# Last group's h on VectorE ahead of P7's T, streamed weights made behind each T's product, and T2 behind k^T v's addition

## The chip, the cores and the metric

The kernel runs on one core of one Trainium2 chip. The metric is the device time in microseconds of one execution. Before the change it is 1124.7 us, the median of three runs (1122.6 to 1124.93). The profile of the kernel before is of one execution and covers 1121.9 us from the first instruction to the last; every time "at" which something happens below is counted from the start of that span.

The core's engines are named as the profile names them: PE is TensorE (matrix products; PEld is its loading of weights), DVE is VectorE, ACT is ScalarE, POOL is GpSimd, and SP is SyncE, which here only issues transfers.

## The reference, cut to what matters

Linear attention with a normalised output is followed by a SwiGLU feed-forward block.

```python
# q, k, v: (8 batches, 8 heads, 576, 64)
kv  = einsum('bhsd,bhse->bhde', k, v)            # k^T v, 64x64 for each head
out = einsum('bhsd,bhde->bhse', q, kv)
out = out / sqrt(mean(out * out, -1) + 1e-6) * g_norm
x   = out.transpose(0, 2, 1, 3).reshape(4608, 512)

# w_gate, w_val: (512, 1536); w_out: (1536, 512)
h = silu(x @ w_gate) * (x @ w_val)
result = h @ w_out
```

Everything is in float32.

## The kernel before: what the change and the steps touch

The 4608 rows of x are cut into nine blocks of 512 (numbered 0 to 8). For each block there is an "up" part (x times the gate and value weights, then h) and a "down" part (h times the output weights). The attention of the next block is computed in between: its k^T v during up, its q transposed between up and down, its products, norm and transposed x during down.

Block 0 does its up part plainly. All other products are done with a seven-product scheme (Strassen's, in Winograd's form) on 2x2 blocks. The seven products are called P1 to P7. Products that go to the same PSUM buffer are accumulated there:

```python
    CHAIN = {1: ("b", True), 6: ("b", False), 7: ("b", False), 4: ("b", False), 2: ("a", True),
             5: ("c", True), 3: ("c", False)}      # PSUM buffer, and whether it begins a sum
```

Three of the weight operands (for P5, P7 and P4) are differences of weight blocks, made on GpSimd and called T. They live in nine buffers (`t_pool`), which are also the buffers into which streamed weights are loaded. T2 is another weight operand, b22 - b12 + b11, made in place.

Block 1 uses one level of the scheme (class `Up`, six units j), and in passing it makes the weights of the second level from the same T and stores them in DRAM. Blocks 2 to 8 use two levels in the up part (class `Inner`: three groups d of four outer products each) and load these weights from DRAM as a stream. The down part always has one level (class `Down`).

The last steps of a group of h in blocks 2 to 8; `HB` is 256 and `BLK` 512:

```python
        def made3(self, p, e, q):                 # class Inner, fourth outer pair (4, 3)
            if p != 4:
                return
            h = self.ffn.h[:, 4 * self.d : 4 * self.d + 4]
            c11, c12, c21, c22 = (self.whole(*i) for i in ((1, 1), (3, 1), (3, 0), (1, 0)))
            mul(nc.gpsimd, h[:, :, 0:HB], c11, c12)
            nc.scalar.activation(out=c21, in_=c21, func=ACT.Silu)
            mul(nc.gpsimd, h[:, :, HB:BLK], c21, c22)
            self.ffn.h_sums(2 * self.d, 2, nc.gpsimd if 4 * self.d + 4 < NF else nc.vector)
```

The down part. P1 reads h's first half, three groups one after the other; P5 reads the sums s1; P7 reads what `turn_s3` leaves in h:

```python
    class Down(Quad):
        ...
        def turn_t(self, p):
            pairs = wo.rearrange("p (j e) d -> p e j d", e=2)
            of = {5: pairs[:, 1, :, HD:DM], 7: pairs[:, 0, :, 0:HD], 4: pairs[:, 1, :, 0:HD]}[p]
            self.t[p] = []
            for i in range(0, NP, 2):
                t = t_tile((self.ffn.n, p))
                sub(nc.gpsimd, t, of[:, i : i + 2], pairs[:, 0, i : i + 2, HD:DM])
                self.t[p] += [t[:, 0], t[:, 1]]
        ...
        def turn_s3(self):
            pairs = self.ffn.h.rearrange("p (j e) t -> p e j t", e=2)
            sub(nc.vector, pairs[:, 0, :, 0:HB], pairs[:, 0, :, HB:BLK], pairs[:, 1, :, HB:BLK])

        def down(self, fill):                     # class Ffn
            down = self.down_
            fill = dict(zip((1, 6, 2), fill))     # steps of the next block's attention
            for p in (1, 5, 6, 7, 2, 4, 3):
                if p == 1:
                    down.turn_t(7)
                if p == 6:
                    down.turn_t(4)
                down.multiply(p)
                self.make(12)
                if p in fill:
                    fill[p]()
                if p == 1:
                    down.turn_s3()
```

The next block's attention: `turn_q` transposes q ahead of P1; the step behind P1 multiplies by k^T v, squares, forms the inverse root (VectorE, eleven small operations) and scales; the step behind P6 begins with `turn_x`, which transposes the scaled x on TensorE.

Block 1's units and what makes the weights of the second level:

```python
    class Up(Quad):
        def sequence(self, last):                 # last: the unit before
            return [(self, 1), (self, 5), (last, 4), (last, 3), (self, 6), (self, 2), (self, 7)]

        def after2(self):
            add(nc.vector, self.s, self.ps["a"], self.s)
            nc.scalar.activation(out=self.s, in_=self.s, func=ACT.Silu)

        def after7(self):
            self.u3 = self.piece(2)
            nc.scalar.copy(out=self.u3, in_=self.ps["b"])
            add(nc.vector, self.u3, self.ps["c"], self.u3)

        def after3(self):
            add(nc.vector, self.u2, self.ps["c"], self.u2)
            mul(nc.gpsimd, self.h[:, :, 0:HB], self.s, self.u2)
            self.ffn.h_sums(self.j, 1, nc.vector)
            if self.ffn.n == DEEP - 1:
                self.ffn.making.extend(leaves(self.j, self.w))
```

`leaves` yields, for each of five sources (three T, and the gate and value weights in pairs), four VectorE operations. It puts all results into one room of 21 blocks of 128x128 (tile xi) and sends a transfer as soon as both of its operands are there, 17 for each unit. Three steps are done after each product in up, twelve in down.

At the end of block 0, behind its down part, the value weights get their T2, and block 1's k^T v has been added up shortly before:

```python
            if js[-1] == NS - 1:                  # Att.kv
                dst = kvs[self.n % 3]
                nc.scalar.copy(out=dst, in_=self.kv_ps[0])
                add(nc.vector, dst, self.kv_ps[1], dst)
    ...
        if n == 0:
            with tc.issue_after(ended.ins):
                for j in range(NP):
                    t2(wv[j][:, 0:2], wv[j][:, 2:4], wg[j][:, 0:2])
```

A scheduler lays down the order in which each engine gets its instructions; the program's order is what it starts from.

Of the kernel before, what the change touches and what calls it, by code (L numbers as in the profile page):

```python
# [8 lines left out]
F32 = mybir.dt.float32  # L9
# [5 lines left out]
P = 128  # L15
# [3 lines left out]
def kernel(  # L19
# [41 lines left out]
    nc = tc.nc  # L61

    B, H, S, D = q.shape
    NT, DM = out.shape
    FF = moe_w_gate.shape[1]
    T = 4
    BLK = P * T
    HB = BLK // 2
    HD = DM // 2
    NB = NT // BLK  # L70
    NS = DM // P
    NF = FF // P
# [12 lines left out]
    x_pool = pool("x", 1)  # L85
# [28 lines left out]
    def ring():  # L114

        return r_pool.tile([P, 4, BLK], F32, name="r")
# [67 lines left out]
    class Att:  # L184
# [57 lines left out]
        def kv(self, js):  # L242


            if self.n == B:
                return
            if js[0] == 0:
                self.kv_ps = [m_psum.tile([P, NS, D], F32, name="m") for _ in range(2)]
            for j in js:
                for c in range(KT):  # L250
                    for r in range(2 if c < KT - 1 else 1):
                        rows = slice(r * D, (r + 1) * D)
                        for u in range(2):
                            nc.tensor.matmul(  # L254
                                self.kv_ps[r][u * D : (u + 1) * D, j, :], lhsT=self.k[j][rows, u, c, :],
                                rhs=self.v[j][rows, u, c, :], start=(c == 0), stop=(c == KT - 1 - r),
                            )
            if js[-1] == NS - 1:
                dst = kvs[self.n % 3]
                nc.scalar.copy(out=dst, in_=self.kv_ps[0])  # L260
                add(nc.vector, dst, self.kv_ps[1], dst)

        def turn_q(self, i, pools=None):

            if i == 0:
                self.qt = ring().rearrange("p t (j c) -> p t j c", j=NS)
            for t in (2 * i, 2 * i + 1):
                pool = pools[t % 2] if pools else m_psum
                ps = pool.tile([P, NS, P], F32, name=pool.name[0])
                for j in range(NS):  # L270
                    nc.tensor.transpose(ps[:, j], self.q[t][:, j], ident)
                if t % 2 or self.n == 1:
                    nc.scalar.copy(out=self.qt[:, t], in_=ps)
                else:
                    nc.vector.tensor_copy(out=self.qt[:, t], in_=ps)
# [103 lines left out]

        def turn(self):  # L380
            for i in range(2):
                self.turn_q(i, (m_psum, b_psum))

        def steps(self):

# [20 lines left out]
    DEEP = 2  # L406

    class Quad:
# [9 lines left out]
        def multiply(self, p):  # L418
            name, first = CHAIN[p]
            if first:  # L420
                self.ps[name] = PSUMS[name].tile([P, 2, HB], F32, name=name)
            for e, i in self.order(p):
                lhsT, rhs = self.operands(p, e, i)

                nc.tensor.matmul(  # L425
                    self.ps[name][:, e], lhsT=lhsT, rhs=rhs, start=first and (e, i) == (0, 0),
                    stop=i == self.steps - 1, skip_group_check=True,
                )
            getattr(self, f"after{p}", lambda: None)()
# [17 lines left out]
    class Up(Quad):  # L447
# [36 lines left out]
        def after3(self):  # L484
            add(nc.vector, self.u2, self.ps["c"], self.u2)
            mul(nc.gpsimd, self.h[:, :, 0:HB], self.s, self.u2)
            self.ffn.h_sums(self.j, 1, nc.vector)
            if self.ffn.n == DEEP - 1:
                self.ffn.making.extend(leaves(self.j, self.w))

    class Inner:

# [100 lines left out]
        def made3(self, p, e, q):  # L593
            if p != 4:
                return
            h = self.ffn.h[:, 4 * self.d : 4 * self.d + 4]
            c11, c12, c21, c22 = (self.whole(*i) for i in ((1, 1), (3, 1), (3, 0), (1, 0)))
            mul(nc.gpsimd, h[:, :, 0:HB], c11, c12)
            nc.scalar.activation(out=c21, in_=c21, func=ACT.Silu)
            mul(nc.gpsimd, h[:, :, HB:BLK], c21, c22)  # L600
            self.ffn.h_sums(2 * self.d, 2, nc.gpsimd if 4 * self.d + 4 < NF else nc.vector)


    RESIDENT = (1, 6, 2, 3)
    QUARTER = {1: (0, 0), 6: (0, 1), 2: (1, 0), 3: (1, 1)}

    CHUNKS = (
        ((5, 1), (5, 6)), ((1, 5), (5, 5)), ((5, 2), (5, 3)), ((1, 7), (5, 7)), ((6, 5), (2, 5)), ((1, 4), (5, 4)),
        ((6, 7), (2, 7)), ((7, 1), (7, 6)), ((7, 7), (7, 5)), ((6, 4), (2, 4)), ((7, 2), (7, 3)), ((4, 1), (4, 6)),
        ((4, 5), (3, 5)), ((7, 4),), ((4, 2), (4, 3)), ((4, 7), (3, 7)), ((4, 4), (3, 4)),  # L610
    )

# [40 lines left out]
        stream.held.append(key)  # L653
        return t_pool.tile([P, 2, 2 * P], F32, name="t")

    made = {}

    def leaves(j, w):


        if not made:
            made["room"] = x_pool.tile([P, 3, 7, P], F32, name="xi").rearrange("p a b c -> p (a b) c")
        room = made["room"]
        d, f = divmod(j, 2)
        two = lambda b: room[:, b : b + 14].rearrange("p (o r) c -> p o r c", o=2)

        sources = []
        for o, b, r in ((5, 1, 2), (7, 18, 1), (4, 12, 2)):
            sources.append((w[o].unsqueeze(1), (o,), room[:, b : b + 2 * r + 1 : 2 * r].unsqueeze(1),
                            room[:, b + r].unsqueeze(1)))  # L670
        for t, os, b in ((wg, (1, 2), 0), (wv, (6, 3), 6)):
            sources.append((t[j].rearrange("p (o i) c -> p o i c", o=2), os, two(b)[:, :, 0:5:4], two(b)[:, :, 2]))
        at = {}
        for o, b, r in ((1, 0, 2), (5, 1, 2), (6, 6, 2), (2, 7, 2), (4, 12, 2), (3, 13, 2), (7, 18, 1)):
            for i, p in enumerate((4, 7, 5)):
                at[o, p] = room, b + i * r
        for o in (5, 7, 4):
            quarters = w[o].rearrange("p i (e c) -> p (i e) c", e=2)
            for i, p in enumerate((1, 6, 2, 3)):
                at[o, p] = quarters, i  # L680
        ready, sent = set(), set()

        def send():
            for c, ops in enumerate(CHUNKS):
                if c in sent or not all(o in ready for o, _ in ops):
                    continue
                sent.add(c)
                src, i = at[ops[0]]
                k = len(ops)
                assert all(at[op][1] == i + m for m, op in enumerate(ops))  # L690
                nc.sync.dma_start(out=stream.dram[d, c][:, 0:k, f], in_=src[:, i : i + k])

        for t, os, t41, t3 in sources:
            t = t.rearrange("p o i (e c) -> p o i e c", e=2)
            b11, t2_, b22 = t[:, :, 0, 0], t[:, :, 0, 1], t[:, :, 1, 1]
            yield lambda b22=b22, t2_=t2_: sub(nc.vector, t2_, b22, t2_)
            yield lambda b11=b11, t2_=t2_: add(nc.vector, t2_, t2_, b11)
            yield lambda t=t, t2_=t2_, t41=t41, n=len(os): sub(
                nc.vector, t41, t[:, :, 1], t2_.unsqueeze(2).to_broadcast([P, n, 2, P])
            )  # L700

            def end(b11=b11, t2_=t2_, t3=t3, os=os):
                sub(nc.vector, t3, b11, t2_)
                ready.update(os)
                send()

            yield end

    class Down(Quad):
        def __init__(self, ffn):  # L710
# [1 line left out]
            self.ffn = ffn  # L712
            self.t = {}

        def turn_t(self, p):
            pairs = wo.rearrange("p (j e) d -> p e j d", e=2)
            of = {5: pairs[:, 1, :, HD:DM], 7: pairs[:, 0, :, 0:HD], 4: pairs[:, 1, :, 0:HD]}[p]
            self.t[p] = []
            for i in range(0, NP, 2):
                t = t_tile((self.ffn.n, p))  # L720
                sub(nc.gpsimd, t, of[:, i : i + 2], pairs[:, 0, i : i + 2, HD:DM])
                self.t[p] += [t[:, 0], t[:, 1]]

        def multiply(self, p):
# [48 lines left out]
    class Ffn:  # L773
        def __init__(self, n, att):
            self.n, self.att = n, att
            self.h = h_pool.tile([P, NF, BLK], F32, name="h")
            self.ps, self.making = {}, []

        def store(self, o, t):
            rows = out[BLK * self.n : BLK * (self.n + 1), :].rearrange("(t p) d -> p t d", t=T)  # L780
# [42 lines left out]
        def down(self, fill):  # L823
            down = self.down_
            fill = dict(zip((1, 6, 2), fill))
            for p in (1, 5, 6, 7, 2, 4, 3):
                if p == 1:
                    down.turn_t(7)
                if p == 6:
                    down.turn_t(4)  # L830
                down.multiply(p)
# [5 lines that stand above are left out]
# [54 lines left out]
    for n in range(NB):  # L891
# [39 lines left out]
            blocks[n + 2].load_kv((0, 1))  # L931
        ffn.down(nxt.steps() if nxt else [])
        if n == 0:
            with tc.issue_after(ended.ins):
                for j in range(NP):
                    t2(wv[j][:, 0:2], wv[j][:, 2:4], wg[j][:, 0:2])

# [30 lines left out]
```

## Time and profile before

| what | value |
|---|---|
| time, median of three | 1124.7 us |
| span of the profiled execution | 1121.9 us |
| mean granted clock of TensorE | 0.968 |
| TensorE busy | 1059.7 us (94%) |
| VectorE busy | 679.9 us (61%) |
| GpSimd busy | 387.2 us (35%) |
| ScalarE busy | 239.0 us (21%) |
| P1 of block 1's down part begins | 266.7 us |
| P1 of the last block's down part begins | 1072.8 us |

The busy shares are averages over parts with different limits. What a change in one part is worth is read from that part: which wait ends last there. A row of a timeline gives the start, the length, the engine, the line of the kernel and the operation, the tile written and the tiles read, and in brackets the idle time before it with what ended that. TensorE's float32 products take two passes, so a product of 12 matrix multiplications stands in the profile as 24.

### The profile page before, as it was taken

The page shows a single profiled execution, that of the slowest core. Times are in us where ns is not written, and L with a number is a line of the kernel's source. Part 1 is how long each engine was busy: PE and PEld are TensorE (multiplying, and loading weights), DVE is VectorE, ACT ScalarE, POOL GpSimd, SP SyncE. Part 2 cuts the span into 40 slices and gives each one's busy share as a digit, 9 for nine tenths or more (in the row PEclk, how much of TensorE's full clock was granted, in tenths as well). Part 3 has the DMA queues.
Part 4 walks back from the last instruction along what each step waited for, and adds up shares of the span by engine and source line. Part 5 has one row for each costly group of instructions (what it writes and reads, how often), then busy time and mean ns, then how long its engine had stood idle before and what let it go on. Part 6 is the DMA issues. An engine that isn't in the chain of part 4 may idle for free.

```text
span 1121.9 us, 21711 instructions
## 1 busy us (share of the span) xinstructions
PE 1059.7 (94%) x8780; PEld 948.6 (85%) x8780; DVE 679.9 (61%) x1241; ACT 239.0 (21%) x380; POOL 387.2 (35%) x294
## 2 busy tenths in 40 slices
PE   4999899888999899989999999989998999899988
PEld 4744688767899889988999899979997999789977
DVE  2999776787556555654655466635664566456631
ACT  2664112111121111212121111211121211121100
POOL 0000432433026701580158104730564046503660
PEclk7899899989999999999999999999998999999989
DMA  9785113574268236831575147624781366036601
GB/s 243 230 264 182 44 43 124 166 186 126 87 199 251 83 84 188 242 103 58 177 238 154 58 135 235 179 60 129 222 232 30 109 186 181 29 91 201 184 2 38
DMA packets 153780, 161.87 MB, mean 144 GB/s; under 512 B 47824, under 2 KB 104528, under 8 KB 153680
## 3 DMA queue, kind: packets, MB, share of 16 engines
q1 hardware_dynamic: 153616, 160.48, 48.6%
q8 instruction: 70, 1.15, 0.4%
q14 instruction: 30, 0.25, 0.1%
q0 software_dynamic: 64, 0.00, 0.0%
HBM read 138.02 MB, written 22.41 MB: 143 GB/s over the span
## 4 chain that ended last, share of the span: by engine, by line
PE 82%; POOL 6%; DVE 5%; DMA 2%; issue 2%; SPq 1%; ACT 1%; POOLq 0%; DVEq 0%
PE b L559 22%; PE b L425 17%; PE c L559 11%; PE c L425 9%; PE a L559 5%; PE a L425 4%; POOL t L111 4%; PE b L849 4%; PE c L849 4%; DVE xi L111 2%; POOL h L112 2%; PE m L338 1%; PE m L291 1%; DMA w<-xi 1%; PE m L254 1%
## 5 line engine op out<-in xcount | busy, mean ns | idle before, releaser
L110 POOL TENSOR_TENSOR r<-r 128x256 f32<-128x256 f32 (+1 forms) x105 | 110.2, 1055 | 420.1 <-DVE r L110 418.5
L110 DVE TENSOR_TENSOR r<-b,r 128x512 f32<-128x512 f32 (+1 forms) x273 | 162.1, 607 | 62.0 <-PE b L559 53.5
L110 DVE TENSOR_TENSOR r<-c,r 128x512 f32<-128x512 f32 (+1 forms) x177 | 108.9, 625 | 101.0 <-PE c L559 56.0
L559 PE MATMUL b<-x,t 128*128 128x128 f32 x1092 | 151.2, 276 | 0.0
L111 POOL TENSOR_TENSOR t<-wo 128x512 f32<-128x512 f32 x81 | 104.1, 1313 | 130.9 <-DVE wo L110 107.1
L112 POOL TENSOR_TENSOR h<-r 128x1024 f32<-128x1024 f32 (+1 forms) x54 | 114.8, 2142 | 83.4 <-DVE r L110 74.9
L559 PEld LDWEIGHTS b<-x,t 128*128 128x128 f32 x1092 | 136.0, 192 | 0.6
L425 PE MATMUL b<-wo,h 128*128 128x256 f32 x432 | 109.7, 412 | 24.2 <-POOL h L112 24.2
L425 PEld LDWEIGHTS b<-wo,h 128*128 128x128 f32 x432 | 88.0, 207 | 40.0 <-POOL h L112 27.0
L110 DVE TENSOR_TENSOR r<-a,r 128x512 f32<-128x512 f32 (+1 forms) x99 | 62.6, 632 | 83.9 <-PE a L559 52.7
L559 PE MATMUL c<-xi,t 128*128 128x128 f32 x840 | 112.1, 275 | 0.0
L559 PEld LDWEIGHTS c<-xi,t 128*128 128x128 f32 x840 | 102.8, 192 | 0.0
L425 PE MATMUL b<-t,h 128*128 128x256 f32 x432 | 97.1, 381 | 0.0
L425 PEld LDWEIGHTS b<-t,h 128*128 128x128 f32 x432 | 80.7, 190 | 11.0 <-ACT r L445 0.2
L573 ACT COPY r<-b 128x512 f32<-128x512 f32 x63 | 36.9, 585 | 218.9 <-PE b L559 184.7
L559 PE MATMUL b<-xi,t 128*128 128x128 f32 x588 | 79.8, 276 | 0.0
L559 PEld LDWEIGHTS b<-xi,t 128*128 128x128 f32 x588 | 72.4, 192 | 0.1
L303 DVE TENSOR_REDUCE z<-r 128x8 f32<-128x512 f32 x36 | 23.1, 680 | 61.3 <-ACT r L302 61.3
L559 PE MATMUL b<-x,wg 128*128 128x128 f32 x336 | 52.9, 280 | 0.0
L559 PE MATMUL b<-x,wv 128*128 128x128 f32 x336 | 51.2, 275 | 0.0
L425 PE MATMUL c<-t,s 128*128 128x256 f32 x216 | 50.4, 390 | 0.0
L425 PE MATMUL a<-wo,h 128*128 128x256 f32 x216 | 48.3, 379 | 0.0
(128 smaller groups left out, 1660.0 us busy)
## 6 DMA issues: line engine op xcount, KB each, us to landing
t<-w SPq DMA_DIRECT2D x336, 256.0 KB, 2.9
out_dram<-r SPq DMA_DIRECT2D x18, 512.0 KB, 3.0
w<-xi SPq DMA_DIRECT2D x60, 128.0 KB, 2.2
ld<-in_q_dram SPq DMA_DIRECT2D x29, 256.0 KB, 4.6
ld<-in_moe_w_gate_dram SPq DMA_DIRECT2D x12, 512.0 KB, 4.8
ld<-in_moe_w_val_dram SPq DMA_DIRECT2D x12, 512.0 KB, 4.8
ld<-in_moe_w_out_dram SPq DMA_DIRECT2D x12, 512.0 KB, 4.6
w<-t SPq DMA_DIRECT2D x36, 128.0 KB, 2.2
```

The lines of the kernel that those rows point to most:

```text
L110: add = lambda e, o, a, b: e.tensor_tensor(out=o, in0=a, in1=b, op=OP.add)
L111: sub = lambda e, o, a, b: e.tensor_tensor(out=o, in0=a, in1=b, op=OP.subtract)
L112: mul = lambda e, o, a, b: e.tensor_tensor(out=o, in0=a, in1=b, op=OP.mult)
L254: nc.tensor.matmul(self.kv_ps[r][u * D : (u + 1) * D, j, :], lhsT=self.k[j][rows, u, c, :], rhs=self.v[j][rows, u, c, :], start=(c == 0), ...
L291: nc.tensor.matmul(self.ps[i][u][p : p + D, t, j, :], lhsT=self.qt[rows, 2 * i + t, j, p : p + D], rhs=kvs[b % 3][rows, j, :], start=True, ...
L303: nc.vector.tensor_reduce(out=self.z[:, i, u], in_=sq, axis=mybir.AxisListType.X, op=OP.add)
L338: nc.tensor.transpose(ps[:, e, t], xt[:, t, j + e], ident)
L425: nc.tensor.matmul(self.ps[name][:, e], lhsT=lhsT, rhs=rhs, start=first and (e, i) == (0, 0), stop=i == self.steps - 1, skip_group_check=True,
L559: nc.tensor.matmul(ps[:, i, f], lhsT=self.weight(o, p, f), rhs=self.operand(o, p), start=first and (i, f) == (0, 0), stop=True, skip_group ...
L573: nc.scalar.copy(out=dst, in_=ps)
L849: nc.tensor.matmul(t, lhsT=w[f // 2][:, i, P * (f % 2) : P * (f % 2 + 1)], rhs=x[:, i, of], start=(i == 0), stop=(i == NS - 1),)
```

## The change

It has three parts.

The last group's h in blocks 2 to 8 (two multiplications and the sums) goes from GpSimd to VectorE; T for P7 waits for the last of these sums, so that GpSimd doesn't work beside them; and the copies of the transposed q go to ScalarE for blocks 3 and later, so that VectorE is free. It is meant to let P1 have h in time.

In block 1 the second-level weights are made behind the product that reads each T, not all behind P3, and the results of the three T go to a ring buffer of their own and those of the gate and value weights to xi. It is meant to give T's buffers back sooner and to take away waits for transfers. Where a transfer's two operands now lie in different rooms it goes as two.

At the end of block 0 the T2 of the value weights waits for the addition of k^T v, and the transposes of block 1's q use PSUM buffer c in place of m.

The diff, cut to its core ("..." marks cuts):

```diff
@@ Att.kv
-                add(nc.vector, dst, self.kv_ps[1], dst)
+                self.kv_made = add(nc.vector, dst, self.kv_ps[1], dst)
@@ Att.turn_q
-                if t % 2 or self.n == 1:
+                if t % 2 or self.n == 1 or self.n > DEEP:
                     nc.scalar.copy(out=self.qt[:, t], in_=ps)
@@ Att.turn
-                self.turn_q(i, (m_psum, b_psum))
+                self.turn_q(i, (c_psum if self.n == 1 else m_psum, b_psum))
@@ Up.after3
-            self.ffn.h_sums(self.j, 1, nc.vector)
-            if self.ffn.n == DEEP - 1:
-                self.ffn.making.extend(leaves(self.j, self.w))
+            self.ffn.ended = self.ffn.h_sums(self.j, 1, nc.vector)
+
+        def multiply(self, p):
+            super().multiply(p)
+            ...
+            if p == 5:
+                self.leaf_room = ring().rearrange("p f (s c) -> p (f s) c", c=P)
+            if p in (5, 7, 4):
+                at = 3 * (5, 7, 4).index(p)
+                ffn.making.extend(leaf_steps(self.j, [(self.w[p].unsqueeze(1), (p,))], self.leaf_room[:, at:]))
+            if p == 3:
+                if ffn.leaf_room is None:
+                    ffn.leaf_room = x_pool.tile([P, 3, 7, P], F32, name="xi").rearrange("p a b c -> p (a b) c")
+                ...
+                ffn.making.extend(leaf_steps(self.j, [(halves(wg), (1, 2)), (halves(wv), (6, 3))], ffn.leaf_room))
@@ Inner.made3
-            mul(nc.gpsimd, h[:, :, 0:HB], c11, c12)
+            engine = nc.gpsimd if 4 * self.d + 4 < NF else nc.vector
+            mul(engine, h[:, :, 0:HB], c11, c12)
             nc.scalar.activation(out=c21, in_=c21, func=ACT.Silu)
-            mul(nc.gpsimd, h[:, :, HB:BLK], c21, c22)
-            self.ffn.h_sums(2 * self.d, 2, nc.gpsimd if 4 * self.d + 4 < NF else nc.vector)
+            mul(engine, h[:, :, HB:BLK], c21, c22)
+            self.ffn.ended = self.ffn.h_sums(2 * self.d, 2, engine)
@@ leaves becomes leaf_steps: the same four operations for each source, then a step that sends
+                if len(ops) == 2 and None not in places and places[0][0] is places[1][0]:
+                    (src, i), (_, k) = places
+                    nc.sync.dma_start(out=dst[:, :, f], in_=src[:, i : k + 1 : k - i])
                     continue
+                for m, place in enumerate(places):
+                    if place:
+                        nc.sync.dma_start(out=dst[:, m, f], in_=place[0][:, place[1]])
@@ Down.turn_t
-        def turn_t(self, p):
+        def turn_t(self, p, after=None):
...
-                sub(nc.gpsimd, t, of[:, i : i + 2], pairs[:, 0, i : i + 2, HD:DM])
+                turned = sub(nc.gpsimd, t, of[:, i : i + 2], pairs[:, 0, i : i + 2, HD:DM])
+                if after:
+                    tc.add_manual_dep(turned.ins, after.ins.name, ...)
@@ Ffn.down
-                    down.turn_t(7)
+                    down.turn_t(7, self.ended)
@@ end of block 0
-            with tc.issue_after(ended.ins):
+            with tc.issue_after(nxt.kv_made.ins), tc.issue_after(ended.ins):
                 for j in range(NP):
                     t2(wv[j][:, 0:2], wv[j][:, 2:4], wg[j][:, 0:2])
```

In the order that the scheduler makes of it, VectorE's sequence in block 1 is nearly the one before; in GpSimd's sequence of a last group the two T of P5 stand ahead of the addition of 128x1024, and the six T of P7 and P4 behind it.

## The prediction

> **What bounds the kernel now.** I read the page's chain of work first, then TensorE's waits, then the timeline around each wait.
>
> ```profile
> PE 1059.7 (94%) x8780; PEld 948.6 (85%) x8780; DVE 679.9 (61%) x1241; ACT 239.0 (21%) x380; POOL 387.2 (35%) x294
> PE 82%; POOL 6%; DVE 5%; DMA 2%; issue 2%; SPq 1%; ACT 1%; POOLq 0%; DVEq 0%
> ```
>
> TensorE (PE) is the bound: 82% of the chain that ends last. What another engine can give back is in the other 18%. TensorE's own waits (us in total, times, longest) say where:
>
> ```profile
> PE b L425 <- POOL h L112: 24.2, 7, 4.9
> PE b L425 <- ACT r L476: 11.3, 3, 4.5
> PE m L271 <- DVE kv L110: 5.3, 1, 5.3
> ```
>
> Each row is one part of the change. The first occurs seven times, once in each of blocks 2 to 8. Block 3 in the timeline (start, length, engine, line):
>
> ```profile
> 485.97 6.20 POOL L111 TENSOR_TENSOR t<-wo 128x512 f32<-128x512 f32 x5
> 492.11 2.40 POOL L110 TENSOR_TENSOR r<-r 128x1024 f32<-128x1024 f32 x1
> 492.20 0.69 DVE L110 TENSOR_TENSOR r<-b,r 128x512 f32<-128x512 f32 x1 [0.41 <-POOL t L111]
> 493.69 3.62 PE L425 MATMUL b<-wo,h 128*128 128x256 f32 x16
> 494.44 3.73 POOL L111 TENSOR_TENSOR t<-wo 128x512 f32<-128x512 f32 x3
> 498.11 4.67 POOL L112 TENSOR_TENSOR h<-r 128x1024 f32<-128x1024 f32 x2
> 500.52 3.78 PE L425 MATMUL b<-wo,h 128*128 128x256 f32 x8 [3.21 <-POOL h L112]
> ```
>
> The last addend of h's last group is there at 492.9 (DVE). GpSimd (POOL) is still at an addition of 128x1024, then makes three T (for P4, needed last), and only then multiplies h. P1 has done the 16 matmuls that need the older groups by 497.3 and stands until 500.5. Its last eight then take 3.78 us; eight of this size take 1.89 in block 1. The table by stretches (length, busy time of PE, PEld, DVE, ACT, POOL, granted clock, DMA) gives the reason in its clock column:
>
> ```profile
> 497.40:500.50 3.10, 0.00 (x0) 0.00 (x0) 0.00 (x0) 0.00 (x0) 3.10 (x3) 0.90 0.00 0
> 500.60:504.30 3.70, 3.70 (x12) 2.51 (x14) 1.38 (x2) 0.00 (x0) 2.17 (x1) 0.50 0.00 0
> ```
>
> The pause is paid again afterwards, at half clock.
>
> The second wait is in block 1, which also makes the streamed weights:
>
> ```profile
> 208.03 1.00 DVE L111 TENSOR_TENSOR xi<-t 128x128 f32<-128x128 f32 x1 [2.15 <-DMA w<-xi]
> 209.40 1.37 DVE L110 TENSOR_TENSOR wg<-wg 128x256 f32<-128x256 f32 x1
> 210.69 0.68 DVE L110 TENSOR_TENSOR r<-a,r 128x512 f32<-128x512 f32 x1
> 211.40 0.63 ACT L472 ACTIVATE r<-r 128x512 f32<-128x512 f32 x1 [9.64 <-DVE r L110]
> 211.94 0.57 ACT L476 COPY r<-b 128x512 f32<-128x512 f32 x1
> 212.56 3.22 PE L425 MATMUL b<-x,t 128*128 128x256 f32 x8 [4.51 <-ACT r L476]
> ```
>
> P2's sum in PSUM a is there at 202.7, but VectorE adds it at 210.69: ahead of it in the queue stand operations that make weights, one waiting 2.15 us for a transfer out of the shared room xi. ScalarE's SiLU waits for the sum, the copy of P7 behind it waits too, and P4 may not add onto b until that copy is done.
>
> The third:
>
> ```profile
> 126.43 0.41 DVE L110 TENSOR_TENSOR kv<-m,kv 128x256 f32<-128x256 f32 x1
> 126.90 1.11 PE L271 MATMUL m<-ident,t 128*128 128x128 f32 x4 [5.29 <-DVE kv L110]
> ```
>
> The k^T v addition stands behind three T2 operations; a transpose needs the PSUM buffer m that it reads, and P1, two matmuls done, stands behind the transpose.
>
> **What the Trainium skill says.** "TensorE: Matmul & The Clock Gate", Part 1 (the HAM clock gate): an idle window of about 3.4 us takes the array to half clock, and it needs about as much activity to return. The trace agrees on the half (0.50) and shows it after only 3.2 us. "SBUF — State Buffer", Who interferes with whom: a VectorE instruction with both inputs in SBUF and a GpSimd instruction reading SBUF shut each other out for a whole instruction; with one input in PSUM they don't. The trace agrees: xi<-wv of 128x512 takes 1.64 us at 203.57, beside a GpSimd multiplication, while xi<-wg of the same size takes 0.68 at 194.02 with GpSimd idle. The clock-gate page also says (Architectural detail) that ScalarE and VectorE are strict first-in-first-out; the 9.64 us above is what that does.
>
> **The change part by part.**
>
> *Last group.* It moves two multiplications of 128x1024 and two sums of 128x512 to VectorE, and two copies of q^T (1.34 us together) from VectorE to ScalarE. T for P7 waits for the last of these sums; T for P4 stands behind it. On VectorE h<-h of 128x1536 takes 1.76 us, so a 128x1024 about 1.2 (an estimate from that row); GpSimd takes 2.3. Take P1's start as 0. The addend ends at -0.8; first multiplication -0.75 to 0.45; P1 needs it at 3.6 (493.69 to 497.3). So three microseconds to spare. ScalarE does one copy of q^T (0.5), then SiLU (1.06) until about 0.6; second multiplication to 1.8; sums (0.65 each) to 3.2. P5 needs their last third late in its run, from 6.4 on. T for P7: from 3.3, done before 9; P7 comes near 19. In GpSimd's order only two T of P5 now stand ahead of the 128x1024 addition instead of five, so that is done near -2. Nothing in this chain reaches TensorE.
>
> What it is worth: from P1's start to P5's start, block 1, which doesn't wait, takes 6.37 us (266.70 to 273.07). Blocks 2 to 7 take 9.86, 12.46, 11.44, 11.50, 12.45 and 11.55: 69.3, against 38.2, so 31.0. Block 8 has no next block's work in between: 12.1 against 5.2, and its P5 6.2 against 5.2: 7.9. Together 39 us, of which 24.2 are the waits and the rest the half clock.
>
> What it costs: six T subtractions (1.25 us each) now run while VectorE forms S3 and the root of the next block's norm. S3 loses some 0.5 us, and three of the root's small two-input operations wait a subtraction out, as at 137.76, 139.34 and 141.06, where each took 1.1 to 1.3 instead of 0.17: 3.1 us. In block 3 the scaling ended at 511.87, 7.6 after P1's end; the transposes that need it come 12.7 after it at the old pace, and near 11.8 at full clock. So 7.6 becomes about 10.5, with some 1 us to spare. I put 2 us for six blocks. Net 37.
>
> *k^T v first.* The addition goes ahead of all T2, so ends near 121.9, and the transposes use PSUM c. P1 then runs 121.4 to 126.6 instead of ending at 134.35: 7.7 us ahead. But VectorE keeps its 12 T2 (mostly 0.62 each), S3, sums and root, and these set when the next block's first x can be turned: in the old run scaling ended at 144.35 and TensorE came at 146.07, only 1.7 later. VectorE can start S3 about 1.8 earlier, loses some of it to GpSimd, and ends near 142.5; TensorE would come at 138.4 and wait 4. Gain 146.07 - 142.5 = 3.5, less 1 for half clock after that wait: 2.5.
>
> *Stream's blocks.* VectorE has as many operations as before, in nearly the same order. The blocks of the three T go to their own ring buffer, those of the weights to xi, so what waited for a transfer out of xi (9.5 us, 8 times) mostly goes. From unit 2 (192.24) to the down product's P5 (273.07) block 1 takes 80.8 us; its matmuls at full clock need 28 + 2 products at 1.73, k^T v 1.4, transposes 1.75, P1 and the next product 6.4: 61.4 us with no wait. Excess 19: 11.8 waits, 6.5 half clock, a little else. Not all of it can go. Per unit, VectorE has some 8.1 us with both inputs in SBUF (three T at four operations of about 0.3, 3.9; two pairs of weights at 1.75; h's sums 0.7), and GpSimd five operations of 1.27 (three T, two of h): 14.5 us that exclude each other, against 12.1 of TensorE. Over four units that is 9.6 late, less the 4 to 5 us by which VectorE may be late unnoticed; with half clock some 8 us stay. And the transfers per unit rise from 17 to 23, six mixed pairs going as two halves; SyncE issues at 0.6 each (0.35 for a half on its own, at 203.75) and had one pause of over 2 us between 186 and 251. I take 8.5 as gain.
>
> Sum: 37 + 2.5 + 8.5 = 48. 1124.7 - 48 = 1076.7.
>
> **Rivals.** (a) *The T subtractions, now late, hold VectorE, and TensorE waits at the next block's transposes instead.* For it: 1 us of slack in my working, and such collisions in the profile. Against: only six subtractions, and the wait is bounded by them. At 3 us a block it takes 18 back, with a clock drop more: 1095 to 1100. (b) *Block 1 gains nothing*, because SyncE's queue or the port shared by VectorE and GpSimd sets it: T's buffers come free later, TensorE waits for T instead of for the copy. For it: SyncE's queue above; VectorE 89% busy from 217 to 239 (19.51 of 22). That makes 1085; if worse than before, 1090. (c) *All three waits go with their half clock*: 39 + 7 + 18, 1061. Against it the exclusive port. (d) *h on VectorE is itself shut out by GpSimd*: only if a T runs in those 4 us, which the added dependency prevents. It would leave perhaps 1 us a block and no pause long enough for the clock: 1084.
>
> **Range and chances.** The 39 us of the last group is measured, and only rival (a) can spoil it; block 1 is uncertain by 8 either way, the handover by 3. Predicted 1077, eight in ten 1066 to 1091. Faster by over 2% means under 1102.2, which needs 22.5 of the 48: 0.95; within 2% 0.04; slower 0.01.
>
> **What would show it.** The wait of P1 for h gone from TensorE's list, P1 in one row of 24 of 5.3 us, no half clock in blocks 2 to 8, their period near 112 instead of 117: the first step right. A wait of the transposes for x (m<-ident,r) for VectorE: rival (a). In block 1 a shorter ACT L476 (its line number moves) and xi waiting no more for transfers, with 5 us of waiting left: the third. New waits for POOL t there: rival (b). Wrong altogether if P1 waits for DVE h for over 2 us a block.

## The result, and the profile after

The changed kernel takes 1077.8 us (median of four, 1074.59 to 1079.33) against 1124.35 us for the kernel before in the same session. The ratio is 0.9585, 95% interval 0.9559 to 0.9611. The predicted time was 1077.0 us.

The profiled execution is the fastest of the four: its span is 1072.7 us, those of the others 1075.0 to 1077.6. Where it and the medians disagree below, the text says so.

On the page after, TensorE's busy row and the chain that ended last, by engine:

```profile
PE 1038.1 (97%) x8780; PEld 935.6 (87%) x8780; DVE 712.7 (66%) x1243; ACT 245.2 (23%) x392; POOL 368.4 (34%) x280
PE 85%; DVE 9%; DMA 2%; SPq 2%; issue 1%; ACT 0%; POOL 0%; DVEq 0%; POOLq 0%
```

TensorE's share of the chain rose from 82% to 85%. GpSimd's 6% is gone from it, and VectorE's share rose from 5% to 9%: most of what is left to gain stands in VectorE's queue. TensorE's waits in the kernel after (us in total, times, longest):

```profile
PE m L338 <- DVE r L112: 9.5, 2, 4.9
...
PE b L425 <- ACT r L476: 6.8, 2, 4.2
...
PE c L425 <- DVE r L110: 1.4, 1, 1.4
```

The wait of P1 for h (24.2 us, seven times) and that of m<-ident for kv (5.3) are not in the list any more. The first row is in part new: one of its two waits, 4.9 us, stands at the kernel's start in the kernel before too, and the other, 4.5, came with the change. The wait for the copy of P7 in block 1 went from 11.3 us (three times) to 6.8 (two), and the one for VectorE's addition there (the last row) from 0.5 to 1.4.

The stretches between four marks on TensorE, read from the two timelines (us):

| stretch | before | after | gain |
|---|---|---|---|
| start to P1 of block 0's down part | 121.0 | 120.5 | 0.5 |
| from there to unit 0 of block 1 (the handover) | 49.1 | 47.0 | 2.1 |
| from there to P1 of block 1's down part (block 1's up part) | 96.6 | 89.3 | 7.3 |
| from there to the end (blocks 2 to 8) | 855.2 | 816.0 | 39.2 |

Of block 1's 7.3 us, 3.6 are waits of TensorE (11.8 before, 8.2 after) and up to 3.4 half clock (13.65 us of it before, 6.83 after; at most half of that is lost).

Block 3 in the timeline of the kernel after, the same place as was shown of the kernel before:

```profile
479.82 2.52 DVE L112 TENSOR_TENSOR h<-r 128x1024 f32<-128x1024 f32 x2
480.51 5.35 PE L425 MATMUL b<-wo,h 128*128 128x256 f32 x24
483.92 8.92 POOL L111 TENSOR_TENSOR t<-wo 128x512 f32<-128x512 f32 x6 [5.56 <-DVE h L111]
...
485.89 2.15 DVE L111 TENSOR_TENSOR h<-h 128x1536 f32<-128x1536 f32 x1 [2.10 <-PE b L425]
489.26 1.16 DVE L309 TENSOR_SCALAR z<-z 128x16 f32<-128x16 f32 x1
490.46 1.19 DVE L312 TENSOR_SCALAR y<-z 128x16 int32<-128x16 int32 x1
491.68 1.19 DVE L319 SCALAR_TENSOR_TENSOR a<-y 128x16 f32<-128x16 f32 x1
...
495.26 0.68 DVE L112 TENSOR_TENSOR r<-a,y 128x512 f32<-128x512 f32 x1
...
497.34 1.04 PE L338 MATMUL m<-ident,r 128*128 128x128 f32 x8
```

P1 is one row of 24, 5.35 us. Both multiplications are over by 482.34. The six T stand in one row behind the sums and cover S3 and the root, of which three small operations take 1.2 us each. The scaling still ends at 495.94, 1.4 us before TensorE's transposes come.

The handover in the kernel after:

```profile
120.46 5.35 PE L425 MATMUL b<-wo,h 128*128 128x256 f32 x24
120.55 0.42 DVE L110 TENSOR_TENSOR kv<-m,kv 128x256 f32<-128x256 f32 x1
...
141.25 0.68 DVE L112 TENSOR_TENSOR r<-a,y 128x512 f32<-128x512 f32 x1
...
141.99 1.88 PE L338 MATMUL m<-ident,r 128*128 128x128 f32 x8 [4.53 <-DVE r L112]
```

P1 no longer stops, but TensorE then waits 4.53 us for the scaled x, and the eight transposes take 1.88 us where block 3's take 1.04. Block 1 in the kernel after:

```profile
207.03 0.52 SPq L705 DMA_DIRECT2D w<-xi  x1
...
210.43 0.42 DVE L111 TENSOR_TENSOR xi<-wg 128x256 f32<-128x256 f32 x1 [4.47 <-DMA w<-xi]
...
223.09 0.68 DVE L110 TENSOR_TENSOR r<-a,r 128x512 f32<-128x512 f32 x1
223.81 0.63 ACT L472 ACTIVATE r<-r 128x512 f32<-128x512 f32 x1 [12.45 <-DVE r L110]
...
224.96 3.78 PE L425 MATMUL b<-x,t 128*128 128x256 f32 x8 [4.22 <-ACT r L476]
```

VectorE still stands for a transfer out of xi, now for 4.47 us in one piece (the first row is where SyncE begins to issue those transfers). Five of its operations between 213.64 and 222.0, beside operations of GpSimd, then take 5.1 us more than such operations take in this block with GpSimd idle (0.32, 0.41 and 0.69 us by size). The sum of P2 comes late, ScalarE and with it P4 behind it, and P4 then runs at half clock.

### The profile page after: what moved, and what is told of

Read it like the earlier page. It is cut to its first block, busy times and chain, and to the rows that moved or that the text cites. A ratio compares the mean times of both kernels' runs of the same rounds, so it can differ in the third digit from the quotient of the medians.

```text
span 1072.7 us, 21807 instructions
## 1 busy us (share of the span) xinstructions
PE 1038.1 (97%) x8780; PEld 935.6 (87%) x8780; DVE 712.7 (66%) x1243; ACT 245.2 (23%) x392; POOL 368.4 (34%) x280
## 4 chain that ended last, share of the span: by engine, by line
PE 85%; DVE 9%; DMA 2%; SPq 2%; issue 1%; ACT 0%; POOL 0%; DVEq 0%; POOLq 0%
PE b L574 25%; PE b L425 16%; PE c L574 12%; PE c L425 8%; PE a L574 6%; PE a L425 5%; PE c L859 4%; PE b L859 4%; DVE xi L111 2%; PE m L338 1%; PE m L254 1%; DVE wv L110 1%; PE m L291 1%; DVE h L111 1%; SPq L222 1%; DVE r L111 1%
## 5 line engine op out<-in xcount | busy, mean ns | idle before, releaser
L111 POOL TENSOR_TENSOR t<-wo 128x512 f32<-128x512 f32 x81 | 116.5, 1464 | 157.7 <-DVE wo L110 107.1
L112 POOL TENSOR_TENSOR h<-r 128x1024 f32<-128x1024 f32 (+1 forms) x40 | 81.9, 2064 | 94.0 <-DVE r L110 80.6
L425 PE MATMUL b<-wo,h 128*128 128x256 f32 x432 | 96.2, 379 | 0.0
L425 PEld LDWEIGHTS b<-wo,h 128*128 128x128 f32 x432 | 81.4, 190 | 10.7
L425 PE MATMUL c<-wo,h 128*128 128x256 f32 x216 | 48.1, 379 | 0.0
```

The source lines that it names most:

```text
L111: sub = lambda e, o, a, b: e.tensor_tensor(out=o, in0=a, in1=b, op=OP.subtract)
L112: mul = lambda e, o, a, b: e.tensor_tensor(out=o, in0=a, in1=b, op=OP.mult)
L425: nc.tensor.matmul(self.ps[name][:, e], lhsT=lhsT, rhs=rhs, start=first and (e, i) == (0, 0), stop=i == self.steps - 1, skip_group_check=True,
```

## The experiments

### Each part alone

**The last group alone**: the kernel before with the changes in `made3`, `turn_q` and `turn_t` (with its wait on `ended`, in block 1 as well), nothing else.

```diff
-            mul(nc.gpsimd, h[:, :, 0:HB], c11, c12)
+            engine = nc.gpsimd if 4 * self.d + 4 < NF else nc.vector
+            mul(engine, h[:, :, 0:HB], c11, c12)
...
-                    down.turn_t(7)
+                    down.turn_t(7, self.ended)
```

> Kernel before with the first part alone (last group's h on VectorE, T for P7 behind its last sum, copies of q on ScalarE). My theory: the three parts are worth what they took from their own stretch of the trace, 39.3 us for this one: 1085, P1 in one row of 24 in blocks 2 to 8, no half clock there. Rival (the parts depend on each other, because GpSimd and VectorE work ahead across blocks): under 35 us, over 1090, with a wait of P1 left.

Measured: 1080.93 us, ratio 0.963 (0.9598 to 0.9663), against 1122.74 for the kernel before: 41.8 us. Blocks 2 to 8 take 815.8 us, as in the whole change. This is a little more than expected: block 1's up part takes 94.1 instead of 96.6, and that is this part's too.

**The stream part alone**: the kernel before with `multiply` of `Up` and `leaf_steps` in place of `leaves`.

```diff
-                self.ffn.making.extend(leaves(self.j, self.w))
...
+            if p in (5, 7, 4):
+                ffn.making.extend(leaf_steps(self.j, [(self.w[p].unsqueeze(1), (p,))], self.leaf_room[:, at:]))
```

> Kernel before with the second part alone (streamed weights made behind each T's product). My theory: 7.3 us, what block 1's up part lost in the trace of the changed kernel: 1117. Rival (a): it gains only with the T2 moved, because VectorE starts the block later: under 3 us, 1121 or more. Rival (b): more than 7.3, over 10, because in the kernel before the waits for xi are longer: under 1114.

Measured: 1119.25 us, ratio 0.9969 (0.9957 to 0.9982), a gain of 3.5 us (2.0 to 4.8). Block 1's up part takes 93.8, 2.8 less than before. So the part does something, about half of what was expected; rival (a), under 3 us, lies within the interval. TensorE's waits in this run:

```profile
PE b L425 <- POOL h L112: 24.4, 7, 5.0
PE b L425 <- ACT r L476: 10.1, 3, 4.2
```

The second row stood at 11.3 before: nearly all of block 1's waits are left.

**T2 behind k^T v alone**:

```diff
-            with tc.issue_after(ended.ins):
+            with tc.issue_after(nxt.kv_made.ins), tc.issue_after(ended.ins):
```

(and `turn` with PSUM buffer c).

> Kernel before with the third part alone (T2 behind the addition of k^T v, transposes of block 1's q in PSUM c). My theory: the wait of 5.3 us goes and one of about 4.5 takes its place behind P6, so 2 us: 1122.3. Rival (the 7.7 us that P1 is ahead are kept): 1117.

Measured: 1121.47 us, ratio 0.9985 (0.9972 to 0.9998); the handover takes 47.4, 1.7 less. The rival, 1117, falls. Gains of the three alone: 41.8 + 3.5 + 1.3 = 46.6, and 46.55 for the whole: by the medians they add up, as far as the interval of the whole (some 44 to 50 us) can tell.

### The last group: engine, order, or wait

**Back on GpSimd, in the new order**: the changed kernel, with both multiplications on GpSimd, the sums and the wait of T as they are.

```diff
-            mul(engine, h[:, :, 0:HB], c11, c12)
+            mul(nc.gpsimd, h[:, :, 0:HB], c11, c12)
```

> Changed kernel with the two multiplications of the last group's h back on GpSimd, ahead of T for P7 and P4 (T still waits for the sums, which stay on VectorE). Theory of order: P1 waited because three T for P4 stood ahead of h, not because GpSimd is slow: from the addend at -0.8 to GpSimd's end at about 1.6 after P1's start, needed at 3.6; no wait, T's end some 2.5 us later, at most 1 us a block lost at the next transposes: 1078 to 1084. Theory of the engine: GpSimd's 2.3 us for a multiplication make P1 wait again, half clock back: 1095 or more.

Measured: 1079.15 us, ratio 0.9612 (0.9575 to 0.9649). This keeps nearly all of the gain (1077.8 with VectorE; the intervals overlap). TensorE's waits:

```profile
PE m L338 <- DVE r L112: 11.7, 9, 4.9
```

P1 doesn't wait. T comes a little later, so that the transposes wait about 0.3 us in seven more places. What cost 24 us before was the place in GpSimd's queue behind three T and an addition, not GpSimd's slower multiplication.

**Without T's wait**: the changed kernel with `down.turn_t(7)`.

> Changed kernel without the dependency of T for P7 on the last sum: three T for P7 go ahead of the addition of 128x1024 on GpSimd, three T for P4 behind it. Theory of exclusion: h's first multiplication on VectorE is shut out by the addition until about 0.8 after P1's start and by a T after it, so takes until 2 to 3.3, still ahead of 3.6: P1 waits for 0 to 1 us in a block, no half clock: 1076 to 1085. Rival (the dependency is what brings the gain): P1 waits for 2 us or more, half clock back: over 1095.

Measured: 1084.35 us (1081.15 to 1090.47), ratio 0.9668 (0.9633 to 0.9704). Its fastest execution was the one profiled: P1 waits once, 2.0 us, in block 2, blocks 2 to 8 take 818.4, and block 1's up part 93.5 in place of 89.3. Most of the gain is there without the dependency, so the rival falls.

**T's wait in blocks 2 to 8 only**, to see whether block 1 owes it 4 us:

```diff
-            self.ffn.ended = self.ffn.h_sums(self.j, 1, nc.vector)
+            self.ffn.h_sums(self.j, 1, nc.vector)
```

> The changed kernel, in which T for P7 waits for the last sum of h in blocks 2 to 8, and not in block 1. Theory (4 us of what block 1 gained come from that wait, although it was made for blocks 2 to 8): from unit 0 of block 1 to P1 of its down part 93.4 us as without the wait anywhere, the rest as in the changed kernel, 1082. Rival (the run without the wait lost those 4 us because of what blocks 2 and later did, or by chance of the order): 89.3 us, 1078.

Measured: 1078.32 us (1077.97 to 1079.12), ratio 0.9601 (0.9574 to 0.9627). The profile says the theory's number, 93.4 us for block 1's up part; in it TensorE waits for T in place of the copy:

```profile
255.30 0.98 PE L425 MATMUL b<-x,t 128*128 128x256 f32 x3 [4.15 <-POOL t L111]
```

The time says the rival's, 1078. Both can be true, since the profiled execution of the changed kernel is the fastest of its four by 2.3 to 4.9 us of span. The profiles side with the theory: block 1's up part takes 89.3 to 90.8 us in all five that keep this wait and the same rooms (the changed kernel, h back on GpSimd, T2 later, and the two of the pauses below), and 93.4 and 93.5 in the two without it. That this doesn't show in the medians stays open, so in time the wait gives block 1 between nothing and 4 us. In blocks 2 to 8 it gives 6 to 7.5 us by the medians (1084.35 against 1078.32; or, each against the kernel before in its own session, a difference of ratios of 0.0067, which is 7.5 of 1124), of which the two profiles show only 2.7 (818.4 against 815.7); the four times without the wait lie 9 us apart.

### Block 1 and the handover: what was left

**T2 of units 1 to 5 later**: only unit 0's T2 directly behind k^T v, the others behind the first half of block 1's scaling.

```diff
-            with tc.issue_after(nxt.kv_made.ins), tc.issue_after(ended.ins):
-                for j in range(NP):
+            for j in range(NP):
+                with tc.issue_after((nxt.kv_made if j == 0 else nxt.scaled0).ins), tc.issue_after(ended.ins):
                     t2(wv[j][:, 0:2], wv[j][:, 2:4], wg[j][:, 0:2])
```

(`scaled0` is the last multiplication of that scaling.)

> Changed kernel with the T2 of units 1 to 5 held until block 1's first scaling is done (unit 0's stays where it is). Theory: VectorE's T2 chain is what delays the scaling, so TensorE's wait of 4.5 us behind P6 of block 0 goes, and about 1.3 us of half clock: 1072. Rival (S3 and the root set it): the wait stays over 3 us, 1077. Rival (T2 is then late for GpSimd's T of units 1 and 2 or for VectorE's next root): a new wait, 1076 or more.

Measured: 1070.41 us, ratio 0.9525 (0.9507 to 0.9544). The handover takes 41.0 instead of 47.0: its wait of 4.53 and the half clock are gone. The T2 ahead of the root in VectorE's queue were the whole of that wait.

**Rooms**: the gate weights' blocks go to the ring buffer beside T's, and the value weights' to three places of xi in turn.

```diff
-                ffn.making.extend(leaf_steps(self.j, [(halves(wg), (1, 2)), (halves(wv), (6, 3))], ffn.leaf_room))
+                ffn.making.extend(leaf_steps(self.j, [(halves(wg), (1, 2))], self.leaf_room[:, 9:]))
+                ffn.making.extend(leaf_steps(self.j, [(halves(wv), (6, 3))], ffn.leaf_room[:, 6 * (self.j % 3):]))
```

> Changed kernel with the gate weights' blocks in the ring buffer beside those of the T, and the value weights' blocks in three places of xi in turn; as many transfers, as many operations. Theory of the room: the wait left in block 1 (6.8 and 1.4 us) comes from VectorE standing 4.5 us for a transfer out of xi at 206 to 210; it goes, and with it the half clock: 6 to 8 us, 1070 to 1072. Theory of exclusion (what I predicted): VectorE and GpSimd shut each other out for longer than TensorE has, so the wait stays: 1076 to 1078.

Measured: 1071.81 us, ratio 0.9539 (0.9518 to 0.9559). VectorE waits for no transfer in block 1 any more (7.0 us, five times, in the changed kernel), block 1's up part takes 84.2 instead of 89.3, and no half clock is left in it. Waits of 5.9 us for the copy are left; the largest:

```profile
222.53 2.00 PE L425 MATMUL b<-x,t 128*128 128x256 f32 x8 [3.27 <-ACT r L476]
```

**Both together**:

> The two before together. If both theories hold and are independent: 1064 to 1067. If the room doesn't matter: 1072.

Measured: 1064.65 us (1064.2 to 1065.25), ratio 0.9475 (0.9458 to 0.9493), as for two independent gains.

**And h of block 1 on VectorE**:

```diff
-            mul(nc.gpsimd, self.h[:, :, 0:HB], self.s, self.u2)
+            mul(nc.vector if self.ffn.n else nc.gpsimd, self.h[:, :, 0:HB], self.s, self.u2)
```

(and the same for the other half of h).

> The version with both mends (T2 of units 1 to 5 held back, two rooms for the weights' blocks), in which the two multiplications of h of each unit of block 1 go from GpSimd to VectorE. It asks what is behind the waits of 5.9 us that remain in block 1. Theory of exclusion (what VectorE and GpSimd do there shuts each other out, so only the sum of both counts): the sum per unit falls by about 1.3 us (two multiplications of 0.65 in place of two of 1.27), the waits shrink to 3 us or less, 1061 to 1063. Rival, theory of VectorE's volume (its own queue is what is late): VectorE has 1.3 us more per unit, the waits grow by 1 to 3 us, 1066 to 1068. GpSimd's own lateness was never seen there, so a gain could only come from exclusion.

Measured: 1058.39 us (1057.22 to 1059.47), ratio 0.9424 (0.9401 to 0.9447), the fastest of all. The rival falls: VectorE got more to do and is less late. It gained more than the theory said, and the version with both mends shows a reason that neither named. Its timeline in block 1:

```profile
210.71 1.26 POOL L112 TENSOR_TENSOR h<-r 128x512 f32<-128x512 f32 x1
212.00 0.43 DVE L111 TENSOR_TENSOR h<-s,h 128x256 f32<-128x256 f32 x1 [2.69 <-POOL h L112]
...
214.60 0.69 DVE L110 TENSOR_TENSOR r<-a,r 128x512 f32<-128x512 f32 x1
```

VectorE's sums need h, whose multiplication stands on GpSimd behind two T. VectorE's whole queue waits 2.69 us for it, with the sum of P2 behind. Five such waits make 8.6 us in block 1. With h on VectorE there is none, and TensorE's waits for the copy are down from 4.5 us to one:

```profile
PE b L429 <- ACT r L480: 1.2, 1, 1.2
```

Exclusion went down as well: xi<-wv of 128x512 took 1452 ns on average there and takes 684 ns here. The run doesn't part these two.

### How a pause turns into time

**P1 made to wait**: the changed kernel, with the first multiplication of the last group five, and then six times over. The result is the same; the repetitions only hold VectorE.

```diff
-            mul(engine, h[:, :, 0:HB], c11, c12)
+            for _ in range(5 if engine is nc.vector else 1):
+                mul(engine, h[:, :, 0:HB], c11, c12)
```

> The changed kernel, in which VectorE does the first multiplication of the last group's h five times over in blocks 2 to 8 (four are useless), which makes P1 wait about 2.0 us in each of the seven. It asks whether a pause must reach a length before the clock halves. Theory of a threshold: 2.0 us are too short, no half clock, the pause costs itself, 7 x 2.0 to 2.4 = 14 to 17, 1092 to 1095. Rival (every pause costs about one and a half times its length, as those of 3.2 us did in the kernel before): 1099 or more, with half clock behind the pauses.

> The same with six times (five useless), which makes P1 wait about 3.3 us in each of the seven blocks. Theory of a threshold: half clock is back behind most of them, at 3.5 to 6.5 us a block as in the kernel before, 25 to 45 in all, 1103 to 1123. Rival (the half clock of the kernel before came from GpSimd's order and not from the pause): only the pauses, 23 us, 1101, and the granted clock stays at 1.0 behind P1.

Measured: 1096.33 us for five (ratio 0.9762, 0.9739 to 0.9784), 1106.7 for six (0.9862, 0.9833 to 0.9892). Neither expectation had the shape of the pause. In the new order the matmuls of q with k^T v fill part of it, and what is left comes in two pieces, one in P1 and one at the transposes. The run with six, blocks 2 and 3:

```profile
378.75 1.99 PE L425 MATMUL b<-wo,h 128*128 128x256 f32 x8 [1.30 <-DVE h L112]
391.65 1.56 PE L338 MATMUL m<-ident,r 128*128 128x128 f32 x8 [2.70 <-DVE r L112]
...
496.18 1.99 PE L425 MATMUL b<-wo,h 128*128 128x256 f32 x8 [1.31 <-DVE h L112]
...
509.08 1.07 PE L338 MATMUL m<-ident,r 128*128 128x128 f32 x8 [2.71 <-DVE r L112]
```

With five, the pieces are 1.34 and 1.41 us and no block from 2 to 7 has half clock. From block 3's P1 to block 4's it takes 114.92 us, 3.16 above 111.76, for 2.75 of pause. With six (4.02 us) it takes 116.19, 4.43 above. So in both a pause costs itself and 0.4. In block 2 of the run with six, after the same 2.70, the clock is halved for 3.41 us (the transposes take 1.56 in place of 1.07); that block is 5.66 above. Of the rivals, the one of a fixed factor falls: a pause without half clock costs hardly more than its length. The one that blamed GpSimd's order falls too, since half clock came without that order. That 1106.7 lies in the range of the theory of a threshold (1103 to 1123) is luck: it is made of pauses, with half clock behind two of them and not behind most. Nor is it the length alone: of six pauses of 2.7 us two were followed by half clock (in blocks 2 and 7), and none of the twelve of 1.3 to 1.4 us of the run with five.

The traces show what it goes with. In each of the fourteen, the granted clock changes only at whole multiples of 3.413 us from its other changes, so time is cut into fixed stretches of that length. Here are the stretch just before block 2's half clock and the emptier of the two that hold block 3's pause (length, TensorE's busy time and matmuls, granted clock, and the transfers' share and rate):

```profile
388.65:392.07 3.42, 0.72 (x6) 1.00 0.00 0
504.71:508.12 3.41, 1.66 (x8) 1.00 0.00 0
```

Block 2's pause lies within one stretch, in which TensorE is busy for only 0.21 of the time; block 3's is cut in two by a border, and its emptier stretch is still 0.49 busy. From 40 us on, all fourteen profiles agree: the clock halved behind all 56 stretches at full clock with a busy share of 0.405 or less, and behind none of the more than 4000 with 0.426 or more. In the first 40 us this doesn't hold: half clock came there behind shares of 0.60 and 0.66 as well.

## Why the prediction was right

**The last group: 39 worked out, 2 deducted, 39.2 measured.** Against P1's start in block 3 the first multiplication begins at -0.7 (predicted -0.75), the second ends at 1.8 (1.8), the sums at 3.3 (3.2), T begins at 3.4 (3.3). The scaling ends 10.1 us after P1's end (10.5) with 1.4 us to spare (1). (The working's terms, 7.6 and 0.5 and 3.1, make 11.2 and not 10.5; what it didn't write down is that VectorE stood idle for 0.80 us before the root in the kernel before, which the longer S3 now fills.) The deduction of 2 us for six blocks was not needed, since that slack held everywhere: from block 2's P1 to block 6's each period is 111.76 us (predicted near 112), with no half clock. Rivals (a) and (d) did not come. The prediction named the order (three T, needed last, ahead of h) and changed the engine as well; the run with h back on GpSimd shows that the order was the cause.

**The handover: 2.5 predicted, 2.1 measured.** The scaling was to end near 142.5 and ended at 141.9; TensorE was to wait 4 and waited 4.53; half clock came, as the 1.88 us of the transposes show. The run with T2 held back shows that the prediction named the right limit: take five of the six T2 away from there and 6 us more come.

**Block 1: 8.5 predicted, 7.3 in the profile, for reasons that were partly others.** The term that was mis-sized is the stream part. Alone it gave 3.5 us, 2.8 of it in block 1's up part. Another 2.5 came there with the last group's part alone, whose T for P7 waits in block 1 too; the prediction didn't count that. The T2 part alone gave nothing there (96.6). The 2.0 that these leave of the 7.3 come from the parts together or from the one execution that was profiled; that stays open. The sign that the prediction named for this step (no waiting for xi, 5 us of TensorE's waits left) didn't come: 7.0 and 8.2 us were left. Two steps of the working failed:

- "What waited for a transfer out of xi (9.5 us, 8 times) mostly goes." It went to 7.0, five times. The blocks of T left xi, but those of the weights kept one room there, and SyncE's queue sends in order: from 194.5 to 199.8 it issues loads of k and v, then what is left of T's blocks, and the transfers out of xi only from 207.0 to 211.1, while VectorE waits from 205.96 to 210.43. The run with more rooms took that wait away and 5.0 us with it.
- The 14.5 us of operations per unit that exclude each other were to explain what stays. They are part of it (the 5.1 us above), but the count left out that VectorE waits for GpSimd's h (3.9 us in the changed kernel, 8.6 with both mends). A count of busy time doesn't show a wait between two queues.

Rival (b) did not come in the changed kernel. Its sign, a wait for POOL t, came in the run where T waits in blocks 2 to 8 only. Rival (c), 1061, could not be had by this change; the three later edits got to 1058. Of what they took away, (c)'s objection had named only the exclusive port, and not the T2 ahead of the root, the room in xi or the wait for h.

The total was right within 1 us of the median. In the profile the three terms were off by +2.2, -0.4 and -1.2 us, which nearly cancel, and the profiled execution gained 49.2 us where the medians gained 46.55. So the mechanisms of the first two terms were right, but that the total fits so closely is in part luck.

## What to carry to other kernels

When TensorE waits for a slower engine, look first at what stands ahead in that engine's queue: moving the work past three T subtractions gave nearly all that moving it to a faster engine gave. Where work is handed from one engine's queue to another and back (here h, for its sums), try it on one of them, even the busier: that gave 6.3 us here, though the hand-over and the exclusion were not parted. And before a room for transfers is shared out anew, look at what the issuing queue does in between: a room that is free on paper is not free until a load ahead has been issued.

## What the runs showed of the hardware

- The cost of a pause on TensorE depends on where it falls. In the kernel before, six pauses of 3.2 us at P1 were followed by no half clock (block 2), by 3.41 us of it (three times) and by 6.83 (twice). Against the same periods from P1 to P1 in the kernel after, that cost 3.5 us, 5.1 to 5.2 us and 6.3 to 6.4 us. Block 2's pause was cut by a border of the fixed stretches of 3.413 us (TensorE was busy for 0.48 and 0.57 of the two). Half clock, too, goes by stretches: from 40 us on in the fourteen profiles, it stayed for one more behind each of the 24 half-clock stretches in which TensorE was busy for 0.81 or less, and ended behind each of the 56 with 0.85 or more. This agrees with the Trainium skill, "TensorE: Matmul & The Clock Gate", Part 1, by which the window that watches activity is free-running and 3413 ns long. The page speaks of an idle window; the runs show that one in which TensorE is busy for 0.40 of the time is enough, and so a pause of 2.70 us, in two of six cases.
- Operations of VectorE that take 0.17 us alone took 1.2 us each beside a row of GpSimd subtractions (1.16, 1.19, 1.19); each ended 0.03 us after one of the subtractions did (at 490.39, 491.62 and 492.84). The prediction took them for two-input operations, of which the Trainium skill says in "SBUF — State Buffer", Who interferes with whom, that they contend with GpSimd's reads. Two of the three, and one of the three that the prediction points at in the kernel before (1.12 us at 137.76), are TENSOR_SCALAR with one tile as input; the page names tensor_scalar among the forms that can take the shared ports, and the trace agrees.
